# A sparse-attention and gated-MLP kernel: K laid out three times by the host and divided in each layout, in place of copies of the divided K from SBUF to SBUF

## The chip, the cores and the metric

The kernel runs on one core of one Trainium2 chip. The metric is the device time of one execution in microseconds. The kernel before was timed three times: 1357.1, 1365.5 and 1371.08 us, median 1365.5 us. The profile shows one further execution whose span is 1362.5 us.

## The reference

```python
def _attn_ref(q, k, v, tau):                       # q, k, v: (8, 8, 576, 64) float32
    scores = scale * np.matmul(q, k.transpose(0, 1, 3, 2))
    thresh = np.max(scores, axis=-1, keepdims=True) - tau
    scores = np.where(scores >= thresh, scores, -1000000000.0)
    ...
    attn = attn / (np.sum(attn, axis=-1, keepdims=True) + 1e-09)
    return np.matmul(attn, v)

def _moe_ref(x, w_gate, w_val, w_out):             # x: (4608, 512), d_ff = 1536
    gate = 1.0 / (1.0 + np.exp(-(x @ w_gate)))
    return gate * (x @ w_val) @ w_out
```

Attention over 8 batches and 8 heads keeps only the scores within tau of the row's maximum; its output, with the heads put side by side, is the input of a gated MLP over 4608 tokens.

## The kernel before, in words

**Number format.** The matrix unit is used in a rounded fp32 format. Where accuracy is needed a float32 tensor is *divided* into a high part (a cast on ScalarE, ACT) and a low part (the tensor minus its high part, mostly on GpSimd, POOL), and products are summed over the parts.

**Attention.** The 64 heads are taken in 32 visits, each a batch b and a pair of heads hp; the names in the rows carry hp, so that kd_1_0 belongs to hp 1, head 0. A visit has nine score tiles (288 columns twice, L661): two of head 0, one of the leftover queries of both heads, two of head 1, two of head 0, two of head 1. A tile's chain runs PE score (L661), DVE maximum (L668), a threshold (L677, on POOL in the first eight visits, then on DVE), ACT exp (L682), DVE mask and sum (L685), PE transposes (L767, L780), ACT copies to SBUF (L718), PE product with V (L803). After a visit its output is scaled on POOL by row sums that went to DRAM and back (rd, rb, L700 to L713). The first three visits use undivided float32 scores (plain_scores); the other 29 use `split_scores`, L562 to L599, which the change rewrites.

**K in `split_scores` before.** A visit loads K once (kn, 128x640, L566): the two heads of the pair lie one above the other on the 128 partitions. ACT casts it to k2's high part (L576), POOL subtracts for the low part (L580). The leftover tile reads k2 itself. The tiles of a single head h need that head twice, in the upper and the lower 64 partitions, with both parts: kd[h], 128x2x640. It is filled by two DMA copies of 64 partitions each from k2 (L597), four a visit. In the same way qd[h] takes the high part of Q in one half and the low part in the other (L593). All these DMAs are issued from one queue, SyncE's (SP).

**The MLP.** Its weights arrive as raw words (wr, L473/L475), are rounded and divided by ACT, DVE and POOL (L483 to L514: wa, wb, ws) and written to DRAM (wid, wod). The matmuls (m L863, o L906) of three blocks of tokens run between the attention's; meanwhile POOL and ACT form sums of weight blocks (s, L957, cast by ACT on L968, subtracted on L969). After the attention six blocks, two at a time, are computed with seven products of such sums in place of eight (L1105, L1170).

**What sets the order.** The functions only declare operations (`op`: engine, estimated cost, key, buffers). `Plan.run` simulates the five engines with these costs, picks at each point the ready operation of lowest key whose buffers have room, and emits all in that order. On the chip every engine then runs its list strictly in order. `SLOTS` says how many buffers a name has; names in `IN_TURN` are handed out in order. A visit is prepared with keys LEAD = 9 tiles ahead.

```python
op("SP", KD_COST, key + h, lambda kd=kd, rows=rows, own=own: nc.sync.dma_start(
    out=f32(kd.ap[rows]), in_=f32(k2.ap[own, :, :SK])
), reads=[k2], writes=[(kd, rows.start)])
```

Of the kernel before, what the change touches and what calls it, by code (L numbers as in the profile page):

```python
# [20 lines left out]
def f32(ap):  # L21
    return ap.bitcast(F32)
# [21 lines left out]
class Plan:  # L44

    IN_TURN = ("x", "xf", "kn", "qn", "vn", "k2", "q2", "kd", "qd", "vs", "p", "pt", "pl", "ptc")

    def __init__(self, pools, slots):  # L50
        self.pools, self.slots = pools, slots
# [3 lines left out]
    def buf(self, tag, shape, dtype, name, cls=None):  # L55
        return Buf(self, tag, shape, dtype, name, cls)
# [166 lines left out]


SLOTS = {
    "kn": 1, "qn": 1, "vn": 1, "k2": 1, "q2": 1, "kd": 3, "qd": 3, "vs": 3,
    "p": 3, "pc": 1, "sm": 8, "st": 16, "pt": 2, "pl": 2, "ptc": 1, "plc": 1, "xf": 2, "rb": 1, "x": 6, "g": 12,
    "w": 9, "t2": 6,
}
# [77 lines left out]
def pool(n):  # L307
    return 0.2 + 0.0022 * n
# [7 lines left out]
def kernel(  # L316
# [36 lines left out]
    SM = NJ * P  # L353
    SL = S - SM
# [80 lines left out]
    op, buf = plan.op, plan.buf  # L435
# [93 lines left out]
    class Visit:  # L529
# [32 lines left out]
        def split_scores(self, key, n):  # L562
            b, hp = self.b, self.hp

            kn = buf("kn", [P, SK], F32, f"kn{n}")
            op("SP", 1.2, key - 4, lambda: nc.sync.dma_start(out=kn.ap, in_=k[b, hp]), writes=[kn])  # L566
# [9 lines left out]
            op("ACT", 0.73, key, lambda: nc.scalar.copy(k2.ap[:, 0, :SK], kn.ap), reads=[kn], writes=[(k2, 0)])  # L576
# [3 lines left out]
            op("POOL", pool(SK), key, lambda: nc.gpsimd.tensor_tensor(  # L580
                out=k2.ap[:, 1, :SK], in0=kn.ap, in1=f32(k2.ap[:, 0, :SK]), op=ALU.subtract
            ), reads=[kn, (k2, 0)], writes=[(k2, 1)])
            op("DVE", 1.4 * W / 640, key, lambda: nc.vector.scalar_tensor_tensor(
                out=q2.ap[:, 1], in0=qn.ap, scalar=scale_t[:, 0:1], in1=f32(q2.ap[:, 0]), op0=ALU.mult, op1=ALU.subtract
            ), reads=[qn, (q2, 0)], writes=[(q2, 1)])
            self.WM = WM
            self.kd, self.qd = {}, {}
            for h in range(2):
                kd = self.kd[h] = buf("kd", [P, 2, SK], F32R, f"kd{n}_{h}")
                qd = self.qd[h] = buf("qd", [P, WM], F32R, f"qd{n}_{h}")  # L590
                own, other = slice(h * D, (h + 1) * D), slice((1 - h) * D, (2 - h) * D)
                for z, rows in enumerate((own, other)):
                    op("SP", 0.5, key + h, lambda qd=qd, rows=rows, own=own, z=z: nc.sync.dma_start(  # L593
                        out=f32(qd.ap[rows]), in_=f32(q2.ap[own, z, :WM])
                    ), reads=[(q2, z)], writes=[(qd, z)])
                for rows in (own, other):
                    op("SP", KD_COST, key + h, lambda kd=kd, rows=rows, own=own: nc.sync.dma_start(  # L597
                        out=f32(kd.ap[rows]), in_=f32(k2.ap[own, :, :SK])
                    ), reads=[k2], writes=[(kd, rows.start)])  # L599
# [584 lines left out]
    def two_blocks(k):  # L1184

        key = 400 + k
        tags = ["x"] * 5 + ["vs"] * 2 + ["k2"] + ["kd"] * 3 + ["p"] * 3
        whole = lambda b: Part(b, lambda: b.ap)
        xt, j = {}, 0
        for prod in SEVEN:  # L1190
            xt[prod] = []
            for c in range(2):
                xt[prod].append(whole(buf(tags[j], [P, 2, SM], F32R, f"xs{k}_{prod}_{c}")))
                j += 1
        base = {}
# [12 lines left out]
        in_two(k, xt, gA, gB)
# [106 lines left out]
def _laid_out(inputs):  # L1315
# [7 lines left out]
    given = {k: _np.ascontiguousarray(x) for k, x in inputs.items()}  # L1323
# [63 lines left out]
```

## Time and profile before

| what | value |
|---|---|
| runs | 1357.1, 1365.5, 1371.08 us |
| profiled execution, span | 1362.5 us |
| PE busy | 1323.1 us (97%) |
| DVE, ACT, POOL busy | 942.9, 726.4, 452.9 us (69%, 53%, 33%) |
| data moved by DMA | 322.37 MB, mean 237 GB/s |
| copies kd<-k | 116 of 320 KB |
| loads of K for the divided visits | 29 of 320 KB |
| last score tile of the attention ends | about 816 us |

The page gives no other time of the profiled execution than its span, so that span is what later sums are made against; it lies 3.0 us under the median of the runs. A row of the windows view gives, for a stretch of the span, its length, then the busy time of PE, of PE's weight load, DVE, ACT and POOL with the number of instructions, then the granted clock, the busy share of the 16 DMA engines and GB/s. A row of the timeline gives start, length, engine, line, operation and, in brackets, the idle time of that engine just before and what ended it. A row of the chain gives start, length, and who had the work at that time.

### The profile page before, as it was taken

How to read it: one execution, taken by the hardware profiler on the slowest of the kernel's cores; microseconds unless marked ns; L12 is line 12 of the kernel's file. 1: busy time of each engine (PE TensorE's matmuls, PEld its weight loads, DVE VectorE, ACT ScalarE, POOL GpSimd, SP SyncE). 2: the span in 40 equal slices, each digit the busy share in tenths (PEclk: the TensorE clock that was granted, in tenths of full speed). 3: DMA queues.
4: the chain of work that ended last, by engine and by line, in shares of the span. 5: the costliest groups of instructions: out<-in, count | busy, mean ns of one | idle time of the engine just before them, and what ended most of it. 6: DMA issues, size and time to landing. Idle time of an engine off the chain costs nothing.

```text
span 1362.5 us, 23334 instructions
## 1 busy us (share of the span) xinstructions
PE 1323.1 (97%) x8290; PEld 1089.2 (80%) x8290; DVE 942.9 (69%) x1848; ACT 726.4 (53%) x1339; POOL 452.9 (33%) x419
## 2 busy tenths in 40 slices
PE   8879999999999998999999999999999999999998
PEld 5557888888877887888878887888888888888887
DVE  7888878677766775677667772746965569655594
ACT  7887777666666765666666552222532225322242
POOL 3575756714444532634544421111000110001100
PEclk9998999999999999999989999999999999999999
DMA  7799999899788787898788777765685656756563
GB/s 267 242 282 312 332 255 284 278 257 263 227 244 248 230 243 224 239 274 260 219 250 261 221 210 244 246 205 188 216 292 195 196 189 219 238 193 190 189 217 123
DMA packets 151612, 322.37 MB, mean 237 GB/s; under 512 B 30152, under 2 KB 57800, under 8 KB 151496
## 3 DMA queue, kind: packets, MB, share of 16 engines
q1 hardware_dynamic: 151352, 320.88, 76.6%
q8 instruction: 66, 1.08, 0.3%
q14 instruction: 50, 0.41, 0.1%
q10 hardware_dynamic: 144, 0.00, 0.0%
HBM read 212.93 MB, written 54.67 MB: 196 GB/s over the span
## 4 chain that ended last, share of the span: by engine, by line
PE 80%; DMA 9%; SPq 4%; ACT 2%; DVE 2%; issue 2%; POOL 2%; POOLq 0%; ACTq 0%; DVEq 0%
PE m L863 11%; PE qb L1105 11%; PE av L803 8%; PE qa L1105 7%; PE qc L1105 7%; PE s L661 7%; PE o L906 6%; PE tp L767 6%; PE rb L1170 5%; PE rc L1170 4%; PE ra L1170 4%; DMA rd<-turned 1%; PE s_l L661 1%; DMA xp<-xf 1%; DMA kd<-k 1%
## 5 line engine op out<-in xcount | busy, mean ns | idle before, releaser
L668 DVE TENSOR_REDUCE st<-s 128x1 f32<-128x576 f32 x256 | 192.2, 752 | 98.7 <-PE s L661 92.1
L685 DVE SCALAR_TENSOR_TENSOR p<-s,st,p 128x576 f32<-128x576 f32 x256 | 207.2, 812 | 45.5 <-ACT p L682 40.5
L682 ACT ACTIVATE p<-s,st 128x576 f32<-128x576 f32 x256 | 191.1, 749 | 32.8 <-DVE st L668 32.2
L718 ACT COPY pt<-tp 128x512 f32<-128x512 f32 x256 | 149.1, 586 | 96.3 <-PE tp L767 95.0
L661 PE MATMUL s<-kd,qd 128*128 128x288 f32 x928 | 169.4, 306 | 5.1 <-DVE p L685 4.3
L863 PE MATMUL m<-x,wi 128*128 128x512 f32 x576 | 165.5, 409 | 1.4 <-ACT pt L718 1.4
L767 PE MATMUL tp<-ident,p 128*128 128x128 f32 x1024 | 157.4, 278 | 7.0 <-ACT xf L718 3.8
L1018 POOL TENSOR_TENSOR gA<-gA 128x512 f32<-128x512 f32 x18 | 24.1, 1341 | 406.8 <-DVE gA L1084 406.8
L661 PEld LDWEIGHTS s<-kd,qd 128*128 128x128 f32 x928 | 141.6, 190 | 20.0 <-DVE p L685 5.7
L767 PEld LDWEIGHTS tp<-ident,p 128*128 128x128 f32 x1024 | 122.1, 142 | 31.3 <-issue 6.4
L803 PE MATMUL av<-pt,vs 128*64 128x256 f32 x1024 | 126.2, 389 | 1.5 <-ACT pt L718 1.3
L906 PE MATMUL o<-g,wo 128*128 128x512 f32 x432 | 119.7, 405 | 0.0
L863 PEld LDWEIGHTS m<-x,wi 128*128 128x128 f32 x576 | 99.4, 190 | 14.5 <-ACT pt L718 1.8
L1105 PE MATMUL qa<-xs_p,wa 128*128 128x512 f32 x432 | 109.5, 389 | 0.0
L803 PEld LDWEIGHTS av<-pt,vs 128*64 128x64 f32 x1024 | 68.6, 138 | 48.5 <-issue 10.2
L1042 DVE TENSOR_TENSOR qu<-qb,qp 128x512 f32<-128x512 f32 x72 | 49.6, 691 | 80.6 <-PE qb L1105 69.3
L1105 PEld LDWEIGHTS qa<-xs_p,wa 128*128 128x128 f32 x432 | 81.1, 188 | 16.8
L906 PEld LDWEIGHTS o<-g,wo 128*128 128x128 f32 x432 | 75.9, 190 | 11.0 <-issue 0.2
L863 PE MATMUL m<-x,ws 128*128 128x512 f32 x288 | 80.4, 412 | 0.6 <-ACT pt L718 0.5
L713 POOL TENSOR_TENSOR xf<-xf,rb 128x576 f32<-128x576 f32 x31 | 44.9, 1448 | 92.0 <-DMA rb<-rd 62.3
L957 POOL TENSOR_TENSOR s<-wi 128x512 f32<-128x512 f32 x24 | 33.0, 1376 | 106.8 <-DMA wi<-wid 101.9
L1010 ACT CAST gs_p<-gA 128x512 fp32r<-128x512 f32 x54 | 32.8, 620 | 61.2 <-DVE gA L1084 23.0
(145 smaller groups left out, 2516.9 us busy)
## 6 DMA issues: line engine op xcount, KB each, us to landing
kd<-k SPq DMA_DIRECT2D x116, 320.0 KB
wi<-wid SPq DMA_DIRECT2D x48, 512.0 KB
wo<-wod SPq DMA_DIRECT2D x36, 512.0 KB
wa<-wid SPq DMA_DIRECT2D x36, 512.0 KB
ws<-sid SPq DMA_DIRECT2D x36, 512.0 KB
wt<-sid SPq DMA_DIRECT2D x36, 512.0 KB
wo_p<-sod SPq DMA_DIRECT2D x36, 512.0 KB
qd<-q SPq DMA_DIRECT2D x116, 128.0 KB
```

Of the source, the lines that this page charges most:

```text
L661: nc.tensor.matmul(s.ap[:, c, :HALF], st(), mv(slice(kc + c * HALF, kc + (c + 1) * HALF)), start=m == 0, stop=m == len(steps) - 1,)
L668: op("DVE", 0.76, key, lambda: nc.vector.tensor_reduce(out=st.ap[:, 0:1], in_=sv(), axis=AX.XY, op=ALU.max, negate=True), reads=[s], write ...
L682: op("ACT", 0.74, key, lambda: nc.scalar.activation(p(), sv(), AF.Exp, bias=st.ap[:, 0:1], scale=1.0), reads=[s, (st, 0)], writes=[(g.p, i)])
L685: op("DVE", 0.9, key, lambda: nc.vector.scalar_tensor_tensor(out=p(), in0=sv(), scalar=st.ap[:, 1:2], in1=p(), op0=ALU.is_ge, op1=ALU.mult ...
L718: return op("ACT", act(n), key, lambda: nc.scalar.copy(dst(), src.ap), reads=[src], writes=[part])
L767: nc.tensor.matmul(tp.ap[:, c, :], self.p.ap[:, o + c * P : o + (c + 1) * P], ident, is_transpose=True, start=c == 0, stop=c == NJ - 1, sk ...
L803: nc.tensor.matmul(av.ap[h * D : (h + 1) * D, a:z], vis.vs.ap[:, j, h], m(h), start=i == 0, stop=i == len(ms) - 1, skip_group_check=True,)
L863: nc.tensor.matmul(m.ap, wv[:, a, c * P : (c + 1) * P], xs[c].ap[:, z, c0:c1], start=e == 0, stop=e == 11,)
L906: nc.tensor.matmul(acc.ap, wv[:, f, a], g[fg * ND + f].ap[:, z], start=(fg, f, a, z) == (0, 0, 0, 0), stop=(fg, f, a, z) == (NFG - 1, ND - ...
L1042: f = lambda: nc.vector.tensor_tensor(out=out.ap, in0=ps_[bank].ap, in1=x.ap, op=ALU.add)
L1105: nc.tensor.matmul(acc.ap, wv[:, y, (2 * h + c) * P : (2 * h + c + 1) * P], xt[prod][c].get()[:, z], start=e == 0 and prod in FIRST, stop= ...
L1170: nc.tensor.matmul(acc.ap, w.ap[:, e, c, y], gt[prod][2 * g + c].get()[:, z], start=m == 0 and g == 0 and prod in FIRST, stop=m == 5 and g ...
```

## The change

The host writes K three times: head 0 in both halves, head 1 in both halves, and the pair as before. The kernel loads each 128x640 piece, casts it on ACT and subtracts on POOL straight into kd[0], k2 and kd[1]; the DMA copies L597 are gone. The pieces' keys are 0, 2 and 3 tiles behind the visit's first. kn has two buffers, where before kn and vn had one each (vn was used only as scratch by the last blocks).

```diff
-    "kn": 1, "qn": 1, "vn": 1, "k2": 1, "q2": 1, "kd": 3, "qd": 3, "vs": 3,
+    "kn": 2, "qn": 1, "k2": 1, "q2": 1, "kd": 3, "qd": 3, "vs": 3,
...
-            kn = buf("kn", [P, SK], F32, f"kn{n}")
-            op("SP", 1.2, key - 4, lambda: nc.sync.dma_start(out=kn.ap, in_=k[b, hp]), writes=[kn])
...
-            op("ACT", 0.73, key, lambda: nc.scalar.copy(k2.ap[:, 0, :SK], kn.ap), reads=[kn], writes=[(k2, 0)])
...
-            op("POOL", pool(SK), key, lambda: nc.gpsimd.tensor_tensor(
-                out=k2.ap[:, 1, :SK], in0=kn.ap, in1=f32(k2.ap[:, 0, :SK]), op=ALU.subtract
-            ), reads=[kn, (k2, 0)], writes=[(k2, 1)])
...
+            for h, at in ((0, 0), (2, 2), (1, 3)):
+                kn = buf("kn", [P, SK], F32, f"kn{n}_{h}")
+                op("SP", 1.2, key - 4 + at, lambda h=h, kn=kn: nc.sync.dma_start(out=kn.ap, in_=k[b, hp, h]), writes=[kn])
+                kd = k2 if h == 2 else buf("kd", [P, 2, SK], F32R, f"kd{n}_{h}")
+                op("ACT", 0.73, key + at, lambda kn=kn, kd=kd: nc.scalar.copy(kd.ap[:, 0, :SK], kn.ap),
+                   reads=[kn], writes=[(kd, 0)])
+                op("POOL", pool(SK), key + at, lambda kn=kn, kd=kd: nc.gpsimd.tensor_tensor(
+                    out=kd.ap[:, 1, :SK], in0=kn.ap, in1=f32(kd.ap[:, 0, :SK]), op=ALU.subtract
+                ), reads=[kn, (kd, 0)], writes=[(kd, 1)])
...
-                for rows in (own, other):
-                    op("SP", KD_COST, key + h, lambda kd=kd, rows=rows, own=own: nc.sync.dma_start(
-                        out=f32(kd.ap[rows]), in_=f32(k2.ap[own, :, :SK])
-                    ), reads=[k2], writes=[(kd, rows.start)])
...
+    k = _np.concatenate([k[..., m:], k], axis=3)
+    heads = k.reshape(b, h // 2, 2, d, -1)
+    given["k"] = _np.stack([_np.concatenate([heads[:, :, i], heads[:, :, j]], axis=2) for i, j in ((0, 0), (1, 1), (0, 1))], axis=2)
```

Because the plan picks by cost and room, every engine's list changes. Three places matter below. The numbers behind a name are a running count that differs between the two kernels; lines of the changed kernel lie some six lower (L578 is its load of kn, L580 its cast, L582 its subtraction).

SP's queue in the third visit, around the load of the raw weight wr_0 (L473, now L472). Before:

```order
L706 DMA rb_0_501<-rd_0_186 64x512
L610 DMA kp_2_1_509<-in_k_dram 128x352
L710 DMA rb_0_501<-rd_0_186 64x64
L706 DMA rb_0_501<-rd_0_186 64x512
L710 DMA rb_0_501<-rd_0_186 64x64
L597 DMA kd_3_0_526<-k_3_457 64x2x640 x2
L566 DMA kn_0_555<-in_k_dram 128x640
L560 DMA vs_3_567<-in_v_dram 128x768
L473 DMA wr_0_569<-in_moe_w_gate_dram 128x1024
```

And now:

```order
L578 DMA kn_3_1_503<-in_k_dram 128x640
L700 DMA rb_0_515<-rd_0_186 64x512
L604 DMA kp_2_1_522<-in_k_dram 128x352
L704 DMA rb_0_515<-rd_0_186 64x64
L700 DMA rb_0_515<-rd_0_186 64x512
L704 DMA rb_0_515<-rd_0_186 64x64
L578 DMA kn_0_0_568<-in_k_dram 128x640
L472 DMA wr_0_574<-in_moe_w_gate_dram 128x1024
```

Ahead of wr_0 the two copies and the load of V are gone, and a load of K stands before the rb rows.

ACT's list at the start of the fifth visit (batch 1, hp 0), when the sixth is prepared. Before, one cast of K stands there, behind the last exp of the visit ahead:

```order
L682 ACTIVATE p_3_12_1190<-s_3_121_1148,st_3_121_1176 128x576
L576 CAST k_1_1230<-kn_1_1104 128x640
L718 COPY pt_3_00_1067<-tp_3_100_1217 128x4x128
L718 COPY pt_3_00_1067<-tp_3_101_1225 128x4x128
L718 COPY pl_3_00_1146<-lk_3_10_1236 128x128
L487 ACTIVATE wb_0_1249<-wr_0_813 128x512
L682 ACTIVATE p_0_00_1254<-s_0_000_1208,st_0_000_1223 128x576
```

And now:

```order
L676 ACTIVATE p_3_12_1161<-s_3_121_1156,st_3_121_1172 128x576
L486 ACTIVATE wb_0_1193<-wr_0_574 128x512
L580 CAST kd_0_1_1199<-kn_0_1_1059 128x640
L676 ACTIVATE p_0_00_1209<-s_0_000_1165,st_0_000_1191 128x576
L712 COPY pt_3_00_1108<-tp_3_100_1201 128x4x128
L580 CAST kd_1_0_1220<-kn_1_0_1175 128x640
L676 ACTIVATE p_0_00_1209<-s_0_001_1186,st_0_001_1197 128x576
```

Two casts stand there, each just ahead of an exp of the running visit; the second reads kn_1_0, whose load the plan starts one score tile earlier. From the eighth visit on the loads start three to seven score tiles ahead of their casts, mostly four or more, counted by the running numbers.

POOL's list around one set of weight sums in the middle of the attention. Before:

```order
L957 TENSOR_TENSOR s_1_0_4454<-wi_1_0_4347 128x512
L887 TENSOR_TENSOR g_0_4482<-th_0_0_4412,g_0_4482 128x512
L580 TENSOR_TENSOR k_2_4541<-kn_2_4291,k_2_4541 128x640
L957 TENSOR_TENSOR s_1_0_4581<-wi_3_0_4460 128x512
L957 TENSOR_TENSOR s_1_0_4454<-s_1_0_4581 128x256
L957 TENSOR_TENSOR s_1_0_4454<-s_1_0_4454 128x256
L957 TENSOR_TENSOR s_1_0_4581<-s_1_0_4454,s_1_0_4581 128x256
L713 TENSOR_TENSOR xf_0_4506<-xf_0_4506,rb_0_4576 128x576
L957 TENSOR_TENSOR s_1_0_4581<-s_1_0_4454 128x256
L969 TENSOR_TENSOR s_1_0_4454<-s_1_0_4454 128x512
```

And now:

```order
L951 TENSOR_TENSOR s_1_0_4520<-wi_3_0_4448 128x512
L582 TENSOR_TENSOR kd_2_0_4518<-kn_2_0_4376,kd_2_0_4518 128x640
L951 TENSOR_TENSOR s_1_0_4255<-s_1_0_4520 128x256
L951 TENSOR_TENSOR s_1_0_4255<-s_1_0_4255 128x256
L951 TENSOR_TENSOR s_1_0_4520<-s_1_0_4255,s_1_0_4520 128x256
L951 TENSOR_TENSOR s_1_0_4520<-s_1_0_4255 128x256
L582 TENSOR_TENSOR k_2_4656<-kn_2_2_4453,k_2_4656 128x640
L963 TENSOR_TENSOR s_1_0_4255<-s_1_0_4255 128x512
L707 TENSOR_TENSOR xf_0_4586<-xf_0_4586,rb_0_4647 128x576
L963 TENSOR_TENSOR s_1_0_4520<-s_1_0_4520 128x512
L582 TENSOR_TENSOR kd_2_1_4736<-kn_2_1_4569,kd_2_1_4736 128x640
```

Subtractions of K (L582) now stand inside the set of sums and around it, three a visit.

More of the change, by code (lines that the diff above doesn't have):

```diff
@@ L44 @@
 class Plan:
-    IN_TURN = ("x", "xf", "kn", "qn", "vn", "k2", "q2", "kd", "qd", "vs", "p", "pt", "pl", "ptc")
+    IN_TURN = ("x", "xf", "kn", "qn", "k2", "q2", "kd", "qd", "vs", "p", "pt", "pl", "ptc")
     def __init__(self, pools, slots):
@@ L285 @@
 FIRST_PAIRS = 4
-KD_COST = 1.2
 TWOS = ((3, 4), (5, 6), (7, 8))
@@ L342 @@
     nc = tc.nc
-    B, NPAIR, P, SK = k.shape
+    B, NPAIR, _, P, SK = k.shape
     D = v.shape[-1]
@@ L563, in split_scores @@
             b, hp = self.b, self.hp
-            kn = buf("kn", [P, SK], F32, f"kn{n}")
-            op("SP", 1.2, key - 4, lambda: nc.sync.dma_start(out=kn.ap, in_=k[b, hp]), writes=[kn])
-            c0, c1 = self.c0, self.c1 + (2 * SL if self.with_left else 0)
-            W, WM = c1 - c0, self.c1 - self.c0
+            W, self.WM = SM + 2 * SL, SM
             qn = buf("qn", [P, W], F32, f"qn{n}")
-            op("SP", 1.2, key - 4, lambda: nc.sync.dma_start(out=qn.ap, in_=q[b, hp, :, c0:c1]), writes=[qn])
-            k2 = self.k2 = buf("k2", [P, 2, SK + P], F32R, f"k2{n}")
-            op("ACT", 0.73, key, lambda: nc.scalar.copy(k2.ap[:, 0, :SK], kn.ap), reads=[kn], writes=[(k2, 0)])
+            op("SP", 1.2, key - 4, lambda: nc.sync.dma_start(out=qn.ap, in_=q[b, hp]), writes=[qn])
             q2 = self.q2 = buf("q2", [P, 2, W], F32R, f"q2{n}")
@@ L585, in split_scores @@
             ), reads=[qn, (q2, 0)], writes=[(q2, 1)])
-            self.WM = WM
+            k2 = self.k2 = buf("k2", [P, 2, SK + P], F32R, f"k2{n}")
             self.kd, self.qd = {}, {}
-            for h in range(2):
-                kd = self.kd[h] = buf("kd", [P, 2, SK], F32R, f"kd{n}_{h}")
-                qd = self.qd[h] = buf("qd", [P, WM], F32R, f"qd{n}_{h}")
+            for h, at in ((0, 0), (2, 2), (1, 3)):
[7 more added lines that the diff above has]
+                ), reads=[kn, (kd, 0)], writes=[(kd, 1)])
+                if h == 2:
+                    continue
+                self.kd[h] = kd
+                qd = self.qd[h] = buf("qd", [P, SM], F32R, f"qd{n}_{h}")
                 own, other = slice(h * D, (h + 1) * D), slice((1 - h) * D, (2 - h) * D)
@@ L593, in split_scores @@
                     op("SP", 0.5, key + h, lambda qd=qd, rows=rows, own=own, z=z: nc.sync.dma_start(
-                        out=f32(qd.ap[rows]), in_=f32(q2.ap[own, z, :WM])
+                        out=f32(qd.ap[rows]), in_=f32(q2.ap[own, z, :SM])
                     ), reads=[(q2, z)], writes=[(qd, z)])
-                for rows in (own, other):
-                    op("SP", KD_COST, key + h, lambda kd=kd, rows=rows, own=own: nc.sync.dma_start(
-                        out=f32(kd.ap[rows]), in_=f32(k2.ap[own, :, :SK])
-                    ), reads=[k2], writes=[(kd, rows.start)])
         def plain_scores(self, key, n):
@@ L1195, in two_blocks @@
         base = {}
-        tags = iter(["qd"] * 3 + ["kn", "qn", "vn"] + ["xf"] * 2)
+        tags = iter(["qd"] * 3 + ["kn"] * 2 + ["qn"] + ["xf"] * 2)
         for hp in (0, 2, 1, 3):
@@ L1333, in _laid_out @@
     given["q0"] = _np.concatenate([q0, q0], axis=1)
-    k = given["k"] = _np.concatenate([k[..., m:], k], axis=3)
+    k = _np.concatenate([k[..., m:], k], axis=3)
+    heads = k.reshape(b, h // 2, 2, d, -1)
+    given["k"] = _np.stack([_np.concatenate([heads[:, :, i], heads[:, :, j]], axis=2) for i, j in ((0, 0), (1, 1), (0, 1))], axis=2)
     k0 = k.reshape(b * h // 2, 2, d, -1)[:NPS].transpose(0, 2, 1, 3)
```

## The prediction

> **What bounds the kernel now.** I read the totals of the page and of the core, then three stretches of the windows view (columns: length; busy time of PE, weight load, DVE, ACT, POOL; clock; DMA share; GB/s).
>
> ```profile
> span 1362.5 us, 23334 instructions
> PE 1323.1 (97%) x8290; PEld 1089.2 (80%) x8290; DVE 942.9 (69%) x1848; ACT 726.4 (53%) x1339; POOL 452.9 (33%) x419
> ```
> ```profile
> core 0: 1362.5 us, clock 0.992
> ```
> ```profile
> 34.00:104.00 70.00, 55.76 (x453) 39.72 (x453) 59.57 (x123) 56.73 (x109) 46.28 (x58) 0.96 0.88 260
> 104.00:340.00 236.00, 235.51 (x1691) 196.94 (x1692) 181.29 (x390) 167.78 (x319) 129.84 (x113) 0.99 0.94 284
> 340.00:816.00 476.00, 460.11 (x3492) 385.77 (x3492) 338.52 (x772) 305.07 (x573) 206.59 (x178) 0.99 0.82 240
> ```
>
> PE is busy 97% of the span and the change adds or removes no matmul, so only PE's idle time and the time lost at a lowered clock can move. Idle are 14.2 us between 34 and 104 us (70.0 - 55.76), 0.5 us up to 340, 15.9 us up to 816; the divided visits lie in these three stretches. The clock's mean of 0.992 costs 0.008 x 1362.5 = 10.9 us. So some 41 us is all that a gain can come from, and 1% of the time is 13.7 us, about what a measurement of this kernel can tell from no change. Which waits make the idle time? The seven largest between 34 and 816 us, from PE's timeline:
>
> ```profile
> 43.61 0.82 PE L653 MATMUL s<-kp,qp 64*128 64x288 f32 x4 [1.70 <-DVE p L685]
> 85.82 0.33 PE L780 MATMUL lk<-ident,p 128*128 128x128 f32 x1 [2.17 <-ACT pt L718]
> 354.58 0.73 PE L863 MATMUL m<-x,wi 128*128 128x512 f32 x2 [1.35 <-ACT pt L718]
> 390.07 0.66 PE L767 MATMUL tp<-ident,p 128*128 128x128 f32 x4 [2.60 <-ACT xf L718]
> 423.94 0.65 PE L767 MATMUL tp_l<-ident,p_l 128*128 128x128 f32 x4 [1.95 <-ACT pt L718]
> 518.90 0.48 PE L780 MATMUL lk<-ident,p 128*128 128x128 f32 x1 [4.54 <-ACT pt L718]
> 683.47 1.33 PE L661 MATMUL s<-kd,qd 128*128 128x288 f32 x4 [3.08 <-DVE p L685]
> ```
>
> They sum to 17.4 us. The chain of waits, followed back from each, passes through a landing DMA; in the same order:
>
> ```profile
> 33.91 7.58 DMA wr<-in_moe_w_gate_dram
> ...
> 41.65 0.80 POOL wa L483
> 42.45 0.25 POOL st L677
> ```
> ```profile
> 76.88 7.03 DMA kd<-k
> ...
> 84.56 0.72 ACT k L576
> ```
> ```profile
> 347.69 2.79 DMA rb<-rd
> ```
> ```profile
> 378.25 5.30 DMA wi<-wid
> ```
> ```profile
> 409.72 6.12 DMA wi<-wid
> ```
> ```profile
> 511.45 6.27 DMA xa<-xa
> ```
> ```profile
> 675.58 2.68 DMA rb<-rd
> ```
>
> The pattern: a DMA lands late, POOL or ACT stands at the head of its list waiting for it, and exps and copies queued behind come late to PE. ACT's two clearest cases:
>
> ```profile
> 387.98 1.14 ACT L968 CAST s<-s 128x512 fp32r<-128x512 f32 x2 [3.46 <-POOL s L957]
> ```
> ```profile
> 517.75 0.62 ACT L813 CAST x<-xa 128x512 fp32r<-128x512 f32 x1 [5.77 <-DMA xa<-xa]
> ```
>
> Of 3.46 and 5.77 us on ACT, 2.60 and 4.54 us reached PE: it has about 1 us of cover. Three of the seven also come with a lowered clock, in these stretches:
>
> ```profile
> 44.00:48.00 4.00, 4.00 (x26) 2.24 (x24) 3.19 (x8) 2.01 (x3) 1.39 (x4) 0.57 0.71 282
> ```
> ```profile
> 510.00:544.00 34.00, 29.46 (x219) 24.30 (x214) 19.38 (x46) 16.55 (x32) 7.56 (x6) 0.95 0.82 233
> ...
> 680.00:714.00 34.00, 30.92 (x210) 25.88 (x209) 21.37 (x48) 21.69 (x41) 17.75 (x16) 0.90 0.85 245
> ```
>
> That is 0.43 x 4 = 1.7, 0.05 x 34 = 1.7 and 0.10 x 34 = 3.4 us.
>
> **The change part by part.** Prices per instruction, from the views of the four lines (min/median/max in ns):
>
> ```profile
> L597 SPq DMA_DIRECT2D kd<-k x116: 603/621/2477, 29.7 to 785.9; - x116
> ...
> L566 SPq DMA_DIRECT2D kn<-in_k_dram x29: 328/1056/1682, 6.4 to 753.2; - x29
> ...
> L576 ACT CAST k<-kn x29: 717/727/742, 23.1 to 774.5; 128x640 fp32r<-128x640 f32 x29
> L580 POOL TENSOR_TENSOR k<-kn,k x29: 1546/1555/2171, 23.9 to 777.6; 128x640 fp32r<-128x640 f32 x29
> ```
> ```profile
> 16.00:20.00 4.00, 4.00 (x28) 2.32 (x30) 4.00 (x10) 3.96 (x10) 2.37 (x5) 1.00 1.03 410
> ...
> 76.00:80.00 4.00, 3.32 (x27) 3.02 (x26) 3.42 (x8) 3.72 (x9) 4.00 (x4) 1.00 1.05 236
> ```
> ```profile
> 60.00:816.00 756.00, 730.14 (x5473) 609.31 (x5472) 559.14 (x1242) 509.76 (x962) 370.23 (x329) 0.99 0.87 255
> ```
>
> *DMA.* A visit loses four copies of 320 KB (1.31 MB) and gains two loads (0.66 MB). Saturated engines (share over 1.0) moved 410 GB/s where only loads ran and 236 GB/s where copies ran among other things. At 410 for both the visit saves 0.66/410 = 1.6 us of DMA time, at 236 for the copies 5.6 - 1.6 = 4.0 us; I take 3 us, since copies were in the slow row. The stretch 60 to 816 us holds the 29 visits, 26 us each, at a share of 0.87: 22.6 us of DMA a visit become about 19.6. What is that worth? The stall at 85.82 goes: its ACT cast waited for the copies out of k2, and no copy reads k2 any more (-2.2). The stall at 43.61 came from wr, queued behind two copies, K and V; now one K stands there and another five DMAs further ahead, net 0.7 MB less, 1.7 us at 410 GB/s. That covers the 1.70 us, and with the gap its clock loss of 1.7 us; I take -3.0. The other five (13.5 us) wait for landings of 2.7 to 6.3 us with a backlog 13% smaller: 0.8 us each, -4, and -1.8 for half the clock loss behind the last. Sum -11; bounds -2.2 (only the direct wait) and -24 (all 17.4 us and the three clock losses, 6.8 us).
>
> *ACT.* Two casts more a visit, 1.45 us, 42 us in all. Between 104 and 816 us ACT is busy 473 of 712 us and PE is full, so 0; without that cover it would be 36 us. Between 34 and 104 us PE has no MLP work and ACT is busy 81%: about six more casts fall there, 4.4 us, while the plan moves a few weight conversions out. Bounds 0 and +4.4, taken +1.5.
>
> *POOL.* Two subtractions more, 3.1 us a visit, 90 us in all; POOL goes from 43% to some 55% between 340 and 816 us. There the sums' casts on ACT (L968) wait for POOL, and a subtraction inside a set adds its length:
>
> ```profile
> 419.30 0.74 POOL L957 TENSOR_TENSOR s<-s,s 128x256 f32<-128x256 f32 x1
> 419.99 1.55 POOL L580 TENSOR_TENSOR k<-kn,k 128x640 fp32r<-128x640 f32 x1
> 421.51 0.73 POOL L957 TENSOR_TENSOR s<-s 128x256 f32<-128x256 f32 x1
> ```
>
> Here 1.55 us of the 1.95 us stall is that subtraction. With the 18 sets of sums that the code declares and three subtractions where there was one, the plan (which knows the 1.6 us) must miss its moment to hurt: bounds 0 and +8 (five sets), taken +2. In the first visits the threshold (L677) stands on POOL between exp and mask: at 66% load, going to about 79%, taken +1, bounds 0 and +4.
>
> *New waits on ACT.* A cast now waits for its own load. In the steady part the load starts mostly four tiles or more ahead, 4 x 26/9 = 11.6 us, against landings of up to 7.6 us: 0. In the fifth and sixth visit it starts one tile ahead at full DMA load; behind that cast stand exps, and PE has nothing else. Bounds 0 and +6, taken +1.5. SP's issue time trades 4 x 0.62 for 2 x 1.06 us: 0.
>
> *DVE.* The low part of Q (L583) takes 0.88 us at best and 1.54 in the median:
>
> ```profile
> L583 DVE SCALAR_TENSOR_TENSOR q<-qn,scale_t,q x29: 881/1539/2283, 24.5 to 776.2; 128x640 fp32r<-128x640 f32 x29
> L685 DVE SCALAR_TENSOR_TENSOR p<-s,st,p x256: 775/810/820, 8.5 to 819.5; 128x576 f32<-128x576 f32 x128
> ```
>
> The mask (L685) never stretches. One L583 a visit stays one, so I add 0; longer ones would fall in DVE's idle time after 104 us. [...]
>
> Sum: -11 + 1.5 + 2 + 1 + 1.5 = -5.0, a span of 1357.5 us. The profiled span lies 3.0 us under the median of the runs, 1365.5, so I expect 1360.5, rounded 1360 us.
>
> **The rivals.** *The backlog was all of it.* If every listed stall follows from late DMAs and the in-order engines keep step otherwise, -24: 1338 in span, 1341 in a run. For it: all seven chains pass through a landing. Against it: the xa wait (4.54 us) had no copy of K just ahead in the queue, and POOL and ACT do get fuller.
>
> *ACT at the head of its list.* 87 casts, each ahead of an exp, wait for a load that waits for a buffer (two of kn) that waits for POOL. If one cast in each visit waits 2 us, PE loses 2 less its 1 us of cover: 29 us; with the sum's -5 +24, 1389 in a run; in every second visit, about 1375; taken 1382. It decides once a landing passes the lead of 11.6 us, or POOL falls behind by as much. For it: ACT's waits above show the price, and a load now needs its buffer back from POOL first. Against it: the DMA queue gets lighter.
>
> *Nothing but noise.* PE is full from 104 us on and both effects hide there: 1363 to 1366. That lies inside my forecast's class. That copies remain is excluded: the changed order holds no copy kd<-k.
>
> **How the numbers follow.** The forecast's class, within 1%, 0.46; all stalls relieved, faster by over 1%, 0.33; ACT waiting, slower by over 1%, 0.21. The likeliest case alone spans 1352 to 1372 (relief twice or none). Down to 1336 and up to 1384 leaves out about 2 in 10, the ends of both rivals.
>
> **What would show it.** Right: no copies; DMA share between 60 and 816 us near 0.76; the waits at 43 and 85 us gone; PE idle of 10 to 12 us between 34 and 104 us and 11 to 16 us between 340 and 816 us; POOL near 540 us and ACT near 768 us busy; PE's busy time unchanged at 1323 us within the clock. Wrong: ACT casts of kd with waits for DMA kn of over 1 us before them in many visits, or idle PE between 104 and 340 us.

## The result and the profile after

The changed kernel takes 1346.61 us (median of 4 runs, 1344.73 to 1348.73), the kernel before 1365.69 us beside it (4 runs, 1357.1 to 1371.08): a ratio of 0.9868, interval 0.9834 to 0.9902. It is faster by 1.3%, 13.4 us under the forecast of 1360: inside its range, but not within 1% of the kernel before, as the forecast had it. Nearest came the rival to which it gave 0.33, that the backlog of DMAs was all of it (1341). A second timing gave 1345.07 us, ratio 0.9852 (0.983 to 0.9874).

First the totals after:

```profile
span 1342.9 us, 23456 instructions
PE 1317.2 (98%) x8290; PEld 1083.4 (81%) x8290; DVE 933.8 (70%) x1848; ACT 758.8 (57%) x1397; POOL 535.7 (40%) x477
```
```profile
core 0: 1342.9 us, clock 0.995
```

The span lost 19.6 us. PE's busy time lost 5.9 us (1323.1 to 1317.2, the same 8290 matmuls at a mean clock of 0.995 instead of 0.992), its idle time 13.7 us (39.4 to 25.7). By stretches, from the windows view of the kernel after:

```profile
34.00:104.00 70.00, 57.88 (x464) 41.29 (x460) 62.20 (x129) 58.49 (x114) 53.81 (x64) 0.95 0.76 248
104.00:340.00 236.00, 234.22 (x1679) 195.14 (x1680) 175.84 (x382) 177.44 (x336) 158.22 (x134) 1.00 0.81 265
340.00:816.00 476.00, 475.40 (x3657) 398.98 (x3654) 338.82 (x791) 332.12 (x620) 254.80 (x211) 1.00 0.69 224
816.00:1335.00 519.00, 516.21 (x2274) 426.23 (x2274) 330.80 (x493) 163.77 (x281) 55.65 (x41) 1.00 0.63 206
```
```profile
60.00:816.00 756.00, 744.65 (x5609) 620.46 (x5608) 554.37 (x1255) 546.33 (x1026) 448.49 (x381) 1.00 0.73 238
```

PE's idle time (length less busy time) went from 14.2 to 12.1 us in the first row, from 0.5 to 1.8 in the second, from 15.9 to 0.6 in the third; in the fourth, where the kernel before was never idle (519.00 of 519.00), it is now 2.8 us. The rows are cut at fixed times, and the attention's last score tile now starts at 802 us instead of 816, so a row does not hold exactly the same work in both kernels. The DMA share of 60 to 816 us fell from 0.87 to 0.73. The gain is thus the third row, and the other rows give a little back. All seven listed stalls are gone. From 34 us on PE's timeline shows only these of more than 0.95 us:

```profile
80.98 0.63 PE L761 MATMUL tp<-ident,p 128*128 128x128 f32 x4 [0.97 <-ACT pt L712]
...
91.22 0.69 PE L761 MATMUL tp<-ident,p 128*128 128x128 f32 x4 [1.12 <-ACT pl L712]
...
828.39 0.51 PE L1099 MATMUL qb<-xs_p,ws 128*128 128x512 f32 x1 [1.31 <-ACT xs_p L1004]
```

The waits view says why. A row tells who waited for what, for how many us in all, how often, and the longest. POOL's sums of weight blocks waiting for their load wi, and ACT's casts waiting for these sums, before and after:

```profile
POOL s L957 <- DMA wi<-wid: 101.9, 20, 9.6
...
ACT s L968 <- POOL s L957: 18.6, 10, 3.6
```
```profile
POOL s L951 <- DMA wi<-wid: 24.5, 9, 5.8
...
ACT s L962 <- POOL s L951: 2.9, 3, 1.0
```

The chain DMA, POOL, ACT, PE on which the prediction rested is broken at its first link: the loads come in time in all but a few cases, although POOL and ACT do more.

### The profile page after: what moved, and what is told of

It is laid out like the page before. It is cut to its first block, busy times and chain, and to the rows that moved or that the text cites. A ratio compares the mean times of both kernels' runs of the same rounds, so it can differ in the third digit from the quotient of the medians.

```text
span 1342.9 us, 23456 instructions
## 1 busy us (share of the span) xinstructions
PE 1317.2 (98%) x8290; PEld 1083.4 (81%) x8290; DVE 933.8 (70%) x1848; ACT 758.8 (57%) x1397; POOL 535.7 (40%) x477
## 3 DMA queue, kind: packets, MB, share of 16 engines
q8 instruction: 66, 1.08, 0.3%
## 4 chain that ended last, share of the span: by engine, by line
PE 92%; DVE 3%; DMA 2%; POOL 1%; ACT 1%; issue 1%; SPq 0%; POOLq 0%; DVEq 0%; ACTq 0%
PE m L857 15%; PE av L797 11%; PE qb L1099 11%; PE s L655 9%; PE tp L761 8%; PE o L900 7%; PE qc L1099 7%; PE qa L1099 7%; PE rb L1164 5%; PE rc L1164 4%; PE ra L1164 4%; PE s_l L655 2%; DVE p L679 1%; PE tp_l L761 1%; PE lk L774 1%
## 5 line engine op out<-in xcount | busy, mean ns | idle before, releaser
L1012 POOL TENSOR_TENSOR gA<-gA 128x512 f32<-128x512 f32 x18 | 24.2, 1342 | 406.8 <-DVE gA L1078 406.8
L857 PE MATMUL m<-x,wi 128*128 128x512 f32 x576 | 161.5, 405 | 0.0
L655 PEld LDWEIGHTS s<-kd,qd 128*128 128x128 f32 x928 | 138.8, 189 | 13.6 <-DVE p L679 3.5
L582 POOL TENSOR_TENSOR kd<-kn,kd 128x640 fp32r<-128x640 f32 x58 | 91.6, 1579 | 67.1 <-ACT kd L580 62.0
L900 PE MATMUL o<-g,wo 128*128 128x512 f32 x432 | 117.0, 403 | 0.0
L900 PEld LDWEIGHTS o<-g,wo 128*128 128x128 f32 x432 | 75.4, 189 | 11.6
L857 PE MATMUL m<-x,ws 128*128 128x512 f32 x288 | 75.2, 400 | 0.0
L582 POOL TENSOR_TENSOR k<-kn,k 128x640 fp32r<-128x640 f32 x29 | 45.2, 1558 | 73.3 <-ACT k L580 73.3
```

What stands on the lines that cost most here:

```text
L582: op("POOL", pool(SK), key + at, lambda kn=kn, kd=kd: nc.gpsimd.tensor_tensor(out=kd.ap[:, 1, :SK], in0=kn.ap, in1=f32(kd.ap[:, 0, :SK]), ...
L655: nc.tensor.matmul(s.ap[:, c, :HALF], st(), mv(slice(kc + c * HALF, kc + (c + 1) * HALF)), start=m == 0, stop=m == len(steps) - 1,)
L857: nc.tensor.matmul(m.ap, wv[:, a, c * P : (c + 1) * P], xs[c].ap[:, z, c0:c1], start=e == 0, stop=e == 11,)
L900: nc.tensor.matmul(acc.ap, wv[:, f, a], g[fg * ND + f].ap[:, z], start=(fg, f, a, z) == (0, 0, 0, 0), stop=(fg, f, a, z) == (NFG - 1, ND - ...
```

## The experiments

Three explanations were set against each other. The traffic: the four copies a visit cost more DMA time than the two loads, and without them all other transfers land earlier. The order: the plan, which simulates the engines with a price for each operation, came out with another and better list, or waits that went with the copies mattered. The prices: the plan takes the DMAs as one serial queue with the price each `op("SP", ...)` names, and stalls come where a transfer takes longer than its price. Where an expectation numbers them, 1 is the traffic, 2 the order and 3 the prices.

### What a copy and a load take

Only DMAs: 16 loads of K, then 16 copies of the form of kd (64 partitions to 64 partitions), 8 copies from DRAM to DRAM, and zeros as output; nothing of the computation is done.

> A kernel that computes nothing: 16 loads of K pieces, then 16 copies of 320 KB as kd's from SBUF to SBUF, then 8 copies of 320 KB from DRAM to DRAM, then zeros as output. The prediction took 3 us of DMA time saved a visit, from bounds of 1.6 (copy as fast as a load, 410 GB/s) and 4.0 us (236 GB/s). Theory 1: a copy takes 1.1 to 1.4 us of the 16 engines against 0.8 us for a load. If copies are as fast as loads: 0.8 us.

```diff
+    for i in range(N):
+        nc.sync.dma_start(out=kns[i], in_=k[i // 4, i % 4, 0])
...
+    for i in range(N // 2):
+        for rows in (slice(0, D), slice(D, P)):
+            nc.sync.dma_start(out=kds[i][rows], in_=k2[(i % 2) * D : (i % 2 + 1) * D, :, :SK])
```

It took 75.19 us. Two stretches with saturated DMA engines, the first with loads alone, the second with copies alone (here the columns are length, busy time of DVE and POOL, clock, DMA share, GB/s):

```profile
9.00:15.00 6.00, 1.19 (x7) 0.00 (x0) 1.00 1.04 404
27.00:39.00 12.00, 0.68 (x4) 0.00 (x0) 1.00 1.05 237
```

At these rates a piece of 320 KB (327,680 bytes) takes 0.81 us as a load and 1.38 us as a copy. A visit thus took 0.81 + 4 x 1.38 = 6.3 us for K and now takes 3 x 0.81 = 2.4: it saves 3.9 us, where the forecast took 3 between bounds of 1.6 and 4.0. The share agrees: 0.14 x 756 us over 29 visits is 3.65 us. The copies from DRAM to DRAM, which two later runs use, moved 364 GB/s between 42 and 46 us, at that rate 0.9 us each:

```profile
42.00:46.00 4.00, 0.17 (x1) 0.00 (x0) 1.00 0.96 364
```

The plan's prices err in opposite directions: 1.2 us for a copy of 1.38, 1.2 us for a load of 0.81. It reckoned 1.2 + 4 x 1.2 = 6.0 us a visit before, 0.3 too little, and 3.6 now, 1.2 too much.

### The kernel before with half the bytes in each copy, in its own order

Each copy takes only the low part of K, and both products of a score read it; the high part is left out of these scores. Order, prices and the number of instructions and DMAs stay.

```diff
-                        out=f32(kd.ap[rows]), in_=f32(k2.ap[own, :, :SK])
+                        out=f32(kd.ap[rows, 1]), in_=f32(k2.ap[own, 1, :SK])
```

> The kernel before with every engine's order unchanged, but only the low part of kd is copied (2 of 4 times 160 KB per head; the scores of single heads use it twice, so the high part is left out). Bytes fall by 0.66 MB a visit, as much as the change saves net; ACT and POOL get no more work. Theory 1, lighter DMA traffic makes the gain: PE idle between 340 and 816 us falls from 15.9 to under 5 us, time 1340 to 1352 us. Theory 2, the new order of the lists makes it: idle stays at 12 to 18 us, time 1360 to 1370 us.

1337.61 us (1335.67 to 1338.95), ratio 0.9798 (0.9767 to 0.9829), a little under the 1340 to 1352 us of the first theory. Its last two attention stretches and its wait for wi:

```profile
104.00:340.00 236.00, 235.90 (x1742) 197.56 (x1741) 180.66 (x389) 168.79 (x320) 133.49 (x115) 1.00 0.79 252
340.00:816.00 476.00, 475.20 (x3599) 399.60 (x3598) 342.60 (x778) 308.35 (x576) 206.05 (x176) 1.00 0.73 227
```
```profile
POOL s L957 <- DMA wi<-wid: 37.0, 11, 5.5
```

With the old order, the copies' waits and no cast or subtraction more, 0.8 us of the 15.9 us of idle time is left. So the traffic alone is enough for the gain; neither a better order nor a removed dependency is needed. This kernel is also 9.0 us faster than the changed one; how much of that is the change's additional work and how much its order, this run does not tell.

### The changed kernel with traffic put back

Copies from DRAM to DRAM, which the plan does not know of, behind the loads of kd[0] and kd[1], with the order of all other operations kept: two a visit, then six (the diff is that of six).

```diff
+            def load_k(h, kn):
+                nc.sync.dma_start(out=kn.ap, in_=k[b, hp, h])
+                for z in range(0 if h == 2 else 3):
+                    nc.sync.dma_start(out=spare_d[n, h, z], in_=k[b, hp, h])
```

> The changed kernel with every order kept, and behind the loads of kd[0] and kd[1] one more DMA each of 320 KB from DRAM to DRAM that nobody waits for: 0.66 MB a visit, the bytes that the change saved. Theory 1 (traffic): the stalls come back, PE idle between 340 and 816 us 8 to 20 us, time 1357 to 1370 us. Theory 2 (order): idle stays under 4 us, time 1344 to 1351 us.

Two copies: 1351.35 us (1348.98 to 1357.24), ratio 0.9909 (0.9877 to 0.9942).

```profile
340.00:816.00 476.00, 473.27 (x3621) 396.44 (x3620) 341.18 (x794) 332.78 (x621) 256.20 (x213) 1.00 0.74 247
```

The share of 60 to 816 us rises from 0.73 to 0.78, idle time in the last stretch from 0.6 to 2.7 us. That is what the theory of the order expected (idle under 4 us); the 8 to 20 us of the traffic theory did not come. But the run puts back less than was meant: the bytes are those that the change saved, the DMA time, by the queue's rows shown below, is 1.3 us a visit of the 3.9. A third of the traffic brought a quarter of the time.

> The changed kernel in its own order, with six copies of 320 KB from DRAM to DRAM a visit that the plan does not know of, behind the loads of the two doubled heads: with two of them the DMA share of 60 to 816 went from 0.73 to 0.78, so six should bring it to about 0.88, what it was before the change. Theory 1 (the traffic that the plan did not reckon with is the cause): the stalls of 340 to 816 come back, PE's idle time there from 0.6 to over 8 us, and the time is 1357 to 1372. Theory 3 (the plan's prices of the DMAs decide, and the bytes only where a plan is too cheap): the same, since these copies have no price at all. The rival that the gain came from the new order itself, or from the waits that went with the copies: below 1353, since neither changes.

Six copies: 1419.84 us (1415.47 to 1422.22), ratio 1.0399 (1.0371 to 1.0427), far above what any theory expected.

```profile
104.00:340.00 236.00, 221.97 (x1532) 181.23 (x1531) 163.42 (x352) 163.76 (x312) 150.26 (x128) 0.98 0.92 317
340.00:816.00 476.00, 445.97 (x3313) 369.92 (x3314) 311.68 (x714) 309.25 (x585) 252.06 (x209) 0.97 0.81 278
```
```profile
POOL s L958 <- DMA wi<-wid: 67.5, 14, 9.3
...
ACT s L969 <- POOL s L958: 34.1, 10, 9.0
...
ACT kd L587 <- DMA kn<-in_k_dram: 18.5, 9, 3.8
```

The stalls are back by the same chain, 30.0 us of idle time in the last stretch and 14.0 in the one ahead of it. One link of it, from the timelines of ACT and PE:

```profile
438.68 0.62 ACT L969 CAST s<-s 128x512 fp32r<-128x512 f32 x1 [8.96 <-POOL s L958]
```
```profile
439.83 0.48 PE L781 MATMUL lk<-ident,p 128*128 128x128 f32 x1 [6.70 <-ACT pt L719]
```

ACT's copy pt stood behind the cast on its list, and PE behind pt. So the new order does not keep the gain, whatever the traffic: the order is there, the gain is not. Whether it would keep a part of it against the old copies at their old price was not run.

The size of the loss has more than one source. The share between 60 and 816 us is 0.85, no more than before the change (0.87), and the time is 55 us longer. But with the stalls the attention ends later, its last score tile starts at 876 us instead of 802, so that stretch holds fewer visits. The queue's row for the whole span (packets, MB, share of the 16 engines) for the kernel before, the change, two copies and six copies:

```profile
q1 hardware_dynamic: 151352, 320.88, 76.6%
```
```profile
q1 hardware_dynamic: 143000, 301.87, 68.8%
```
```profile
q1 hardware_dynamic: 144856, 320.88, 71.2%
```
```profile
q1 hardware_dynamic: 148568, 358.90, 75.2%
```

Times the spans that is 1043.7, 923.9, 960.9 and 1065.4 us of the engines: 0.64 us a copy with two and 0.81 us with six. Six put back 4.9 us a visit, more than the 3.9 that the change saved (4.1 by these rows). Besides, the plan knows nothing of these copies, and the casts wait for loads behind them. The run does not tell the three apart.

### The kernel before with a dearer copy

All copies stay; the plan takes 1.8 instead of 1.2 us for each, so only the order moves.

```diff
-KD_COST = 1.2
+KD_COST = 1.8
```

> The kernel before with the plan's price of a kd copy at 1.8 in place of 1.2 us: the copies stay, only the order of the lists moves. Theory 1 (traffic): time within 8 us of before, 1358 to 1373 us. Theory 2 (order, the plan took the copies for too cheap): 1345 to 1356 us.

1354.35 us (1349.8 to 1358.0), ratio 0.9936 (0.9908 to 0.9964).

```profile
104.00:340.00 236.00, 229.83 (x1645) 190.88 (x1646) 174.71 (x374) 163.59 (x310) 124.78 (x108) 0.99 0.93 273
340.00:816.00 476.00, 474.65 (x3628) 400.24 (x3627) 341.47 (x793) 313.58 (x584) 207.67 (x180) 1.00 0.90 255
```
```profile
POOL s L957 <- DMA wi<-wid: 4.1, 2, 3.2
...
ACT s L968 <- POOL s L957: 1.2, 1, 1.2
```

With the whole traffic, and a share even higher than before (0.90 against 0.82 from 340 to 816 us), the idle time there falls from 15.9 to 1.35 us and the waits for wi from 101.9 to 4.1 us. So a DMA share of 0.90 did not stall PE by itself here. The time lies in the 1345 to 1356 us of the second theory. That the better price did it is not shown: a new price gives new lists throughout, and this is one of them (another price, of the load, loses 24 us below). The stretch ahead pays for it with 6.2 us of idle time (0.5 before), 3.6 us of them up to 116 us, since the MLP's first matmul now starts at 114.5 us instead of 104.3. So less remains than the change brings.

### The changed kernel with other prices of the load

```diff
-                op("SP", 1.2, key - 4 + at, lambda h=h, kn=kn: nc.sync.dma_start(out=kn.ap, in_=k[b, hp, h]), writes=[kn])
+                op("SP", 2.0, key - 4 + at, lambda h=h, kn=kn: nc.sync.dma_start(out=kn.ap, in_=k[b, hp, h]), writes=[kn])
```

> The changed kernel, only the plan's price of a load of K is 0.4 in place of 1.2 us, so the lists are ordered for loads that land sooner than they do; bytes and work are the same. Theory 3, stalls come where a DMA lands later than the plan reckoned: PE idle between 340 and 816 us rises from 0.6 to 4 to 15 us, time 1351 to 1365 us. Theory 1, only the bytes count: idle stays under 2 us, time 1342 to 1350 us.

> The changed kernel, only the plan's price of a load of K is 2.0 in place of 1.2 us. Theory 3: a plan on the safe side keeps PE idle between 340 and 816 us under 2 us, time 1340 to 1352 us, what moves being the stages before 340 us. If any shift of the order is as good as a throw of dice: over 1355 or under 1338 us.

> The changed kernel once more, so that the two kernels after it can be set against it on one chip. Every theory: about 1346.6 us, its median so far, within some 3 us.

> The changed kernel with a price of 2.0 us for each load of K, once more and beside the changed kernel on one chip. If the price is worth what it seemed: 1335 to 1339, 8 to 11 us below the changed kernel's own time on this chip, and PE idle for under 1 us from 816 on. If it was the chip: within 4 us of it.

> The changed kernel with a price of 2.8 us for each load of K in the plan, instead of 1.2 (0.4 gave 1349, 1.2 gave 1346.6, 2.0 gave 1337). If a dearer load makes the plan better because it holds work back until its data are there: 1334 to 1340. If 2.0 was one good draw among orders: anything from 1336 to 1356, and the idle time is in another place than at 1.2.

| price of a load | time, us | ratio (interval) | PE idle 34-104, 104-340, 340-816, 816-1325 |
|---|---|---|---|
| 0.4 | 1349.12 | 0.9904 (0.9866-0.9943) | 12.8, 1.3, 0.2, 3.9 |
| 1.2 (the change) | 1346.61 | 0.9868 (0.9834-0.9902) | 12.1, 1.8, 0.6, 2.8 |
| 1.2, again | 1345.07 | 0.9852 (0.983-0.9874) | 13.4, 1.3, 0.4, 2.9 |
| 2.0 | 1337.06 | 0.981 (0.9758-0.9861) | 12.0, 0.2, 0.0, 0.0 |
| 2.0, again | 1335.84 | 0.9791 (0.9766-0.9816) | 11.6, 0.2, 0.2, 0.0 |
| 2.8 | 1371.0 | 1.0059 (1.0029-1.009) | 13.3, 3.3, 7.3, 11.2 |

The last column ends at 1325 us because the shortest of these spans ends at 1336.8. The rows "again" ran on one chip: 9.2 us apart, with intervals that do not touch. So the changed kernel with 2.0 beats both kernels. But no rule stands behind the number. The first run at 2.0 came out under the 1340 to 1352 us of the theory of the prices, in the range put down for a throw of dice. At 0.4 a load takes 2 times its price, and yet between 104 and 816 us no stall is over 0.7 us: with the share at 0.73 a price that is too low did no harm there, against what the theory of the prices expected. (Its largest stall, 3.69 us at 87 us, comes from DVE; it is shown further below.) At 2.8 both expectations were missed, 1334 to 1340 by 31 us and 1336 to 1356 by 15. There the attention ends later (its last score tile starts at 832 us instead of 802), and the MLP's matmuls that could fill PE's gaps are used up: the last of L900 starts at 783 us. Up to 700 us PE is never idle; all 7.3 us of the third stretch lie behind.

```profile
340.00:700.00 360.00, 360.00 (x2690) 301.74 (x2689) 239.09 (x549) 248.68 (x470) 224.60 (x192) 1.00 0.73 232
```
```profile
340.00:816.00 476.00, 468.70 (x3517) 392.29 (x3516) 322.90 (x753) 323.67 (x603) 257.09 (x213) 1.00 0.72 228
816.00:1335.00 519.00, 507.80 (x2328) 418.59 (x2328) 338.09 (x523) 171.20 (x295) 62.18 (x46) 0.99 0.61 200
```
```profile
853.55 0.80 PE L1099 MATMUL qb<-xs_p,ws 128*128 128x512 f32 x1 [7.58 <-ACT xs_p L1004]
```

The 7.58 us is the stall that the change brings at 828 us (1.31 us, shown above), grown. In the repeated 2.0 it is gone, and 106 matmuls of the MLP stand behind the attention there; the change's own plan has 30 left. From PE's timelines, the repeated 2.0 and then the change:

```profile
795.55 24.34 PE L900 MATMUL o<-g,wo 128*128 128x512 f32 x106
```
```profile
813.86 7.10 PE L900 MATMUL o<-g,wo 128*128 128x512 f32 x30
```

The other runs bear this out in the main. With 70 left (the kernel before, the half copies) and with 82 (SLACK 6, below) there is no such stall. With 30 (the change, its DRAM copies, the short casts) it is 1.08 to 1.44 us, with 36 (the copy at 1.8) 1.20 us and with none 7.58 us. With 42 (the load at 0.4) it is 3.23 us, so the number left does not set its size alone.

### Shorter casts, and another spread of the MLP

Casts and subtractions of kd cover 288 of 640 columns; the other columns are left out and the scores read the first ones instead. DMAs and order are those of the change.

```diff
-    lambda kn=kn, kd=kd: nc.scalar.copy(kd.ap[:, 0, :SK], kn.ap),
+    lambda kn=kn, kd=kd, m=m: nc.scalar.copy(kd.ap[:, 0, :m], kn.ap[:, :m]),
```

> The changed kernel with its order kept, but the casts and subtractions of kd[0] and kd[1] cover 288 of 640 columns, and the scores of single heads read these 288 twice (the other columns of K are left out). It takes about 0.3 us of ACT and 0.8 us of POOL from each of 58 pieces. If the added ACT and POOL work cost 4.5 us as predicted: 1342 to 1345 us. If it hides wholly: 1345 to 1348 us, within 0.2% of the changed kernel.

1342.72 us (1341.86 to 1343.96), ratio 0.9837 (0.9807 to 0.9868). POOL is busy for 491.5 us instead of 535.7, ACT for 744.2 instead of 758.8.

```profile
34.00:104.00 70.00, 57.39 (x473) 40.61 (x471) 63.03 (x133) 60.69 (x120) 52.83 (x66) 1.00 0.75 253
104.00:340.00 236.00, 235.88 (x1697) 196.66 (x1698) 175.41 (x382) 171.10 (x333) 145.46 (x134) 1.00 0.80 265
```

The idle time of 104 to 340 us falls from 1.8 to 0.1 us, that of 34 to 104 us does not (12.6). So with half of ACT's and POOL's additional work taken away 1.2 to 1.7 us less idle time is left there (the change's two profiles have 1.8 and 1.3). The time lies in the 1342 to 1345 us that stood for a cost of 4.5 us, but the gain of 2 to 4 us is not told apart from the change by the intervals. The load at 2.0, with all of this work, is idle for 0.2 us there: whether the work reaches PE depends on the order.

Last, SLACK is the number of MLP units by which a visit may run ahead of an even spread.

```diff
-RATE, SLACK = 3, 3
+RATE, SLACK = 3, 6
```

> The changed kernel with SLACK 6 in place of 3: a visit of the attention may start three weight loads' worth of MLP work earlier, so that more of it is left over behind the last visit. If the idle time between 816 and 835 us (2.8 us) comes from having too little MLP work left there, it goes: 1341 to 1345 us; if the new order costs elsewhere what it gains: 1345 to 1352 us.

1351.76 us (1348.47 to 1355.53), ratio 0.9928 (0.9903 to 0.9954).

```profile
104.00:340.00 236.00, 227.17 (x1632) 186.54 (x1634) 174.78 (x383) 176.73 (x331) 152.17 (x125) 1.00 0.78 253
...
816.00:1335.00 519.00, 519.00 (x2291) 429.92 (x2290) 328.57 (x491) 164.27 (x283) 54.37 (x41) 1.00 0.65 213
```

The stall behind the attention goes (519.00 of 519.00), and 8.8 us of idle time appear between 104 and 340 us: cover is moved, not made.

### What the runs say together

For each kernel the DMA time of K that the plan reckons for a visit, what it takes by the measured prices (a half copy as half of 1.38; the DRAM copies 0.64 us each with two and 0.81 with six, from the queue's rows), the share between 60 and 816 us, and PE's idle time from 340 to 816 us:

| kernel | reckoned | takes | share | idle |
|---|---|---|---|---|
| before | 6.0 | 6.3 | 0.87 | 15.9 |
| before, half copies | 6.0 | 3.6 | 0.76 | 0.8 |
| before, copy at 1.8 | 8.4 | 6.3 | 0.91 | 1.35 |
| change | 3.6 | 2.4 | 0.73 | 0.6 |
| change, two DRAM copies | 3.6 | 3.7 | 0.78 | 2.7 |
| change, six DRAM copies | 3.6 | 7.3 | 0.85 | 30.0 |
| change, load at 0.4 | 1.2 | 2.4 | 0.73 | 0.2 |
| change, load at 2.0 | 6.0 | 2.4 | 0.74 | 0.0 |
| change, load at 2.8 | 8.4 | 2.4 | 0.75 | 7.3 |

Two rows have large idle time behind late DMAs: the kernel before and the six DRAM copies. In both the share is 0.85 or more and the plan reckons with less than the transfers take. The half copies, with the old order and less traffic, take the idle time away; so does the copy at 1.8, with the old traffic and another order. The change does both: it saves 3.9 us of DMA time a visit, and a load that the plan prices too high stands where a copy was priced too low.

That less traffic is enough is shown by the half copies. That a wrong price is the other half of the cause is argued, not shown. The kernel before is short by only 0.3 us a visit, and with the same shortfall and a share of 0.94 its PE is idle for just 0.5 us between 104 and 340 us. Also, every new price moves all lists at once. The 7.3 us at 2.8 are of another kind: there PE has run out of MLP work, and no late DMA is needed for it.

## Why the prediction was right and wrong

**The number.** The forecast was a gain of 5 us, the measured one is 19. The range held because it was made to reach the first rival, not because the forecast's sum was right.

**What bounds the kernel: right.** PE stayed at 1317.2 of 1342.9 us, and what moved was idle time and clock, 13.7 and 5.9 us.

**DMA, -11: the step that failed.** The DMA time saved, 3 us a visit, measured 3.9, and its share 0.73 where 0.76 was forecast: small. What failed is "a backlog 13% smaller: 0.8 us each, -4, and -1.8 for half the clock loss". It let the lateness of the five later stalls shrink in proportion to the backlog. (Worked out, 13% of the five landings is 3.0 us in sum, not 4, and half of 3.4 is 1.7: the step was a little too high by its own rule.) In fact, with the bytes of the copies halved, the idle time between 340 and 816 us fell to almost nothing (15.9 to 0.8 us), and so it did with another order (1.35 us). In the change it fell by 15.3 us, and the clock rose from 0.99 to 1.00, where -5.8 was forecast for both. A likely reading, not shown by a run of its own, is that lateness is what a transfer takes beyond what the lists allow, a small difference of large numbers, so that a small cut can remove all of it. The argument that the xa wait had no copy just ahead of it in the queue did not hold: that stall is gone in the change and also in the half copies, which keep the old order.

**The stalls at 43 and 85 us: right in place, too large in sum.** Both are gone, the lowered clock at 44 to 48 us too (0.57 before, 1.00 now), but the stretch of 34 to 104 us lost 2.1 us of idle time where -5.2 was forecast with the clock; others of about 1 us stand there now. Its mean clock did not rise (0.96 before, 0.95 now), for a lowered clock now stands at its end:

```profile
92.00:104.00 12.00, 10.16 (x74) 7.60 (x74) 10.32 (x22) 9.43 (x19) 8.65 (x8) 0.73 1.04 372
```

In all runs this stretch is idle for between 10.9 us (the half copies) and some 15 us (SLACK 6), so less traffic took at most 3.4 us off the 14.2.

**ACT +1.5, POOL +2 and +1: wrong in place, the sum not settled.** ACT rose by 32 us and POOL by 83, against 42 and 90 forecast. The sums' casts, where +2 was put, wait less than before (2.9 us against 18.6), since their data are early. The additional work shows in 104 to 340 us (0.5 to 1.8 us of idle time), which the forecast took as covered; shorter casts took that back, and so did the load at 2.0 with all of the work. So no run shows a cost of 4.5 us that comes with this work in every order. (The 36 us that ACT's casts would cost without cover comes out as some 38, 42 less 4.4; the sum did not use it.)

**New waits for the loads, +1.5: too high.** No cast of K waits for kn in the change, so the second rival (1382) did not happen. Its mechanism exists: six DRAM copies a visit brought nine such waits, 18.5 us in all. What the casts do wait for is their buffer:

```profile
ACT kd L580 <- PE s L655: 20.1, 30, 1.8
```

30 times ACT stood until PE had read the last kd, up to 1.8 us, which no step of the prediction had; PE's total shows little of it.

**Left out: the cover behind the attention.** In the kernel before, PE had this run of MLP matmuls when the attention had ended:

```profile
827.99 16.17 PE L906 MATMUL o<-g,wo 128*128 128x512 f32 x70
```

The plan now puts 40 of them ahead of the attention's end, the 30 left (7.10 us, above) do not cover what the next blocks wait for, and 2.8 us of idle time follow. The load at 2.0, without this, and with 0.2 us in place of 1.8 between 104 and 340 us, comes within the runs' scatter of the half copies.

**DVE, 0: right for the change's time; the instruction got shorter.** L583 is now L570:

```profile
L570 DVE SCALAR_TENSOR_TENSOR q<-qn,scale_t,q x29: 876/885/2018, 25.8 to 765.8; 128x640 fp32r<-128x640 f32 x29
```

Its median fell from 1.54 to 0.885 us though POOL has three subtractions where it had one. Before, the plan put it beside POOL's subtraction, as at 294 us:

```profile
293.62 1.56 POOL L580 TENSOR_TENSOR k<-kn,k 128x640 fp32r<-128x640 f32 x1 [4.27 <-ACT k L576]
```
```profile
294.31 1.55 DVE L583 SCALAR_TENSOR_TENSOR q<-qn,scale_t,q 128x640 fp32r<-128x640 f32 x1 [0.53 <-DMA wo<-wod]
```

POOL had 0.87 us to go when it started; it took 0.67 us longer than its 0.88 and ended 0.68 us behind POOL's. Now Q is divided before K's pieces come, and in 17 of 29 visits no instruction of POOL overlaps it (in one of 29 before); these all take 0.88 or 0.89 us. Of the 12 that one overlaps, six take 0.88 or 0.89 us too and six 1.03 to 2.02 us; no run shows what tells the two apart. The 0 held with most of the overlap gone. That is the luck of this order. In the run with the load at 0.4, L570 once met three POOL instructions in a row, two of them subtractions of K, and PE stood until DVE came to the next mask:

```profile
80.72 4.99 DVE L570 SCALAR_TENSOR_TENSOR q<-qn,scale_t,q 128x640 fp32r<-128x640 f32 x1
```
```profile
87.42 1.33 PE L655 MATMUL s<-kd,qd 128*128 128x288 f32 x4 [3.69 <-DVE p_l L679]
```

With SLACK 6 it happened too (5.58 us, and 3.02 us of PE). So a long L570, which the prediction took for 0, did reach PE in these two orders.

## What to carry to other kernels

Where in-order lists come from a plan, set the plan's price of each transfer against its measured time, and ask of a stall whether the transfer behind it was late or only reckoned early. Another price can remove a stall as well as fewer bytes do, but it is a draw: here 2.0 won 9 us and 2.8 lost 24. A stall behind a busy queue need not shrink in proportion to the traffic: here a cut of the DMA share by a sixth (0.87 to 0.73) took nearly all of it (15.9 to 0.6 us of idle time between 340 and 816 us), so let the upper bound of such a term take all of it, and give that bound weight. And look at the cover that is left behind a stage after the plan has moved, since work that fills a gap early is missing later.

## What the hardware showed that was not expected

In the run that only moves data a copy from 64 partitions of SBUF to 64 partitions moved 237 GB/s with all DMA engines busy (share 1.05), a load into 128 partitions 404 GB/s (share 1.04), so by these rates a copy of the same bytes cost 1.7 times a load. No run here copies 128 partitions from SBUF to SBUF, so whether the partitions or the source set the rate is not shown.

With six DRAM copies a visit the same 8290 matmuls were busy for 1338.1 us at a mean clock of 0.981, 20.9 us more than in the change at 0.995, and PE was idle for 78.7 us (1416.8 less 1338.1) instead of 25.7. The clock did not follow the idle time in every run: with SLACK 6 it was 0.997 at 32.3 us idle (1349.8 less 1317.5).

```profile
PE 1338.1 (94%) x8290; PEld 1092.8 (77%) x8290; DVE 936.3 (66%) x1848; ACT 756.6 (53%) x1397; POOL 536.1 (38%) x477
```
